# Two token blocks with attention beside them: where the scores lie, when the softmax and the stores run, and how early the next stage's weights are loaded

## The chip, the core and the metric

The kernel runs on one core of one Trainium2 chip. Its engines are TensorE (PE in the profile, its weight loads PEld), VectorE (DVE), ScalarE (ACT), GpSimd (POOL) and SyncE (SP, which issues nearly all DMAs here). The metric is the device time of one execution in microseconds (us), the median of several runs.

## The reference

Pooled attention, a gated layer and a second layer with a rational activation, all in float32:

```python
# q, k, v: 8 batches x 8 heads x 576 tokens x 64
k_p = k.reshape(B, H, Sp, 8, D).mean(axis=3)          # 72 pooled keys, v_p likewise
scores = scale * q @ k_p^T;  scores -= max(scores)
attn = exp(scores) / (sum(exp(scores)) + 1e-09)
x = (attn @ v_p)            # as 4608 tokens x 512
# gated layer, 512 -> 1536 -> 512
x = (silu(x @ w_gate) * (x @ w_val)) @ w_out
# second layer, 512 -> 2048 -> 512
h = x @ w_in;  P = a0 + a1 h + a2 h^2 + a3 h^3
Q = 1 + |b0||h| + |b1| h^2;  out = (P / (Q + 1e-06)) @ w_out2
```

## The kernel before, in words

The 4608 tokens are nine blocks of 512. The hidden width 1536 of the gated layer is twelve tiles `f` of 128. Every float32 product is done as three matmuls on a high and a low part (`mm3`), so a gate product `gp` or a value product `vp` of one tile is 12 matmuls of 128x512.

Stages in order of time: block 0 (35 to 158 us) also turns the weights into parts; blocks 1 and 2 (158.7 to about 355 us) run `gp` and `vp` for each tile; then three pairs of blocks run with fewer products (`ca`, `cb`, `cc`, 12 steps `n` each, to 775 us), which read sums of weights (`sw`) back from DRAM; then the output products, and from 950 us the second layer.

Attention for later blocks runs in between, in units of up to 128 tokens: block 2's during tiles 4 to 9 of block 1, that of blocks 3 and 4 during block 2. A unit goes: load `q` (`qload`); scores `sc` on PE; in the next tile the softmax read on DVE (`soft1`, L380 and L383, twice), the exponential on ACT (`soft_exp`, L393), sum and division (`soft2`, L405 to L408; the division on DVE or, with `helped`, on GpSimd), a copy (`soft3`, L416, GpSimd); in the tile after that PE transposes the result (`t`, L433 and L437), ACT and DVE copy it (`ptr` L440 and L445, `pt` L441), and PE multiplies by the pooled values (`pv`, L461 and L464), which ACT copies to `xraw` (L470).

The order is written by hand. `attention_slots` puts each step into a `plan` by tile and place; the loop over tiles calls the places: "0" ahead of `gp`, "A" behind the silu (L789), "B" ahead of the gated product `hh * vp` (L803), "B2" behind its store (L811), "C" at the end. All engines take their instructions in that order, so an instruction that waits holds up what stands behind it on its engine, and on SP a store that waits holds up the loads behind it. `prepare(2)` loads pieces of `k` and `v` and reduces them (L291, L309) in the same tile. `sum_weights`, `sum_splits` and `sum_store` work every second tile on the weight sums of the pair stage (`rs`, `ws`, stores `sd`, `wd`, `vd`). `stream(n, ...)` loads the pieces `sw` of step `n`; `token_sums` and `token_part` make the parts `x0b11`, `x0t1`, ... of the first pair on DVE and ACT.

PSUM has eight banks: four `ps_acc` (block 0's outputs, later the pair products), two `ps_gv` (`gp` and `vp`), two `ps_at` (scores, transposes and `pv` take turns). SBUF slots of 36 (`wslot`) hold weights and much else and are handed on as they come free.

Of the kernel before, what the change touches and what calls it, by code (L numbers as in the profile page):

```python
# [19 lines left out]
P = 128  # L20
# [44 lines left out]
def attention_gated_rational(  # L65
# [279 lines left out]

    SCALE = 1.0 / (POOL * math.sqrt(D))

    def scores(u, qt, early=False, helped=False, heads=False):

        b, s, n, o = u
        kr = st["kr", b]
        if early:
            w = wslot(f"p{b}_{s}", (P, 2 * 512), F32)
            pt = w[:, : H * SP].rearrange("p (h s) -> p h s", s=SP)
            pr = w[:, H * SP : H * SP + 6 * RG].rearrange("p (c r i s) -> p c r i s", c=2, r=3, i=2)
        else:
            pt = at.tile([P, H, SP], F32, tag="p", name=f"p{b}_{s}", bufs=2)  # L360
            pr = at.tile([P, 2, 3, 2, REST], F32, tag="pr", name=f"pr{b}_{s}")
        mx = at.tile([P, 2, NPAIR], F32, tag="mx", name=f"mx{b}_{s}", bufs=2)
        sm = at.tile([P, H], F32, tag="sm", name=f"sm{b}_{s}", bufs=2)
        banks = []
        for half in range(2):
            sc = bank(f"sc{b}_{s}_{half}", min(s // P, 2) if early else None)
            banks.append(sc[:, : 4 * SP].rearrange("p (c s) -> p c s", s=SP))

        for c in range(NPAIR):
            for half in range(2):  # L370
                rows = slice(half * D, (half + 1) * D)
                nc.tensor.matmul(  # L372
                    banks[half][:n, c, :], qt[rows, c * n : (c + 1) * n], kr[rows, c * SP : (c + 1) * SP],
                    start=True, stop=True,
                )

        def soft1():
            for half in range(2):
                sc = banks[half]
                nc.vector.tensor_reduce(mx[:n, half], sc[:n], axis=AX.X, op=ALU.max)  # L380
                if heads:
                    continue
                nc.vector.tensor_tensor(  # L383
                    pt[:n, half::2], sc[:n],
                    mx[:n, half].unsqueeze(2).to_broadcast([n, 4, SP]), op=ALU.subtract,
                )

# [98 lines left out]
    def attention_slots(js, start, helped=False, heads=False):  # L486


        def put(slot, place, fn):
            plan.setdefault((slot, place), []).append(fn)  # L490

        groups = [g for j in js for g in units(j)]
        owner = [j for j in js for g in units(j)]
        box = {}
        fl = [(g, i) for g in range(len(groups)) for i in range(len(groups[g]))]

        def do_xraw(j):
            if j > PLAIN and (j - PLAIN) % 2:
                st["xraw", j] = [wslot(f"xraw{j}_{i}", (P, 2, BLK), F32) for i in range(2)]
            else:  # L500
                t = keep.tile([P, KT, BLK], F32, tag="xraw", name=f"xraw{j}")
                st["xraw", j] = [t[:, 0:2, :], t[:, 2:4, :]]
        for n, (g, i) in enumerate(fl):
            u = groups[g][i]
            slot = start + n
            put(slot - 1, "B2", lambda u=u: box.__setitem__(("q", u), qload(u)))
            put(slot, "C", lambda u=u: box.__setitem__(("s", u), scores(u, box.pop(("q", u)), False, helped, heads)))
            put(slot + 1, "A0" if slot + 1 >= PLAIN * NF1 else "0", lambda u=u: box["s", u][0]())
            put(slot + 1, "0" if heads else "A", lambda u=u: box["s", u][1]())
            put(slot + 1, "B" if js[0] >= PLAIN else "B2", lambda u=u: [fn() for fn in box.pop(("s", u))[2:]])  # L510

            def t_(u=u, g=g, i=i, at_bank=0 if slot + 2 >= PLAIN * NF1 else None):
                if i == 0:
                    box["pt", g] = new_pt(f"{js[0]}_{g}")
                for fn in transposes(u, box["pt", g], i * P, at_bank):
                    fn()
            put(slot + 2, "A", t_)
            if i + 1 == len(groups[g]):
                def v_(g=g):
                    j = owner[g]  # L520
                    if ("xraw", j) not in st:
                        do_xraw(j)
                    values(groups[g], box.pop(("pt", g)), st["xraw", j])
                    if g + 1 < len(groups) and groups[g + 1][0][0] != groups[g][0][0]:
                        build_vs(groups[g + 1][0][0])
                put(slot + 2, "B", v_)
# [104 lines left out]

    def sum_weights(f):

        rg, rv = sums_w[f] = [ldp.tile([P, 2, QUART], F32, tag="ld", name=f"r{x}{f}") for x in "gv"]
        for r, w in zip((rg, rv), (W1[f"g{f}"], W1[f"v{f}"])):
            nc.vector.tensor_tensor(r.rearrange("p h c -> p (h c)"), f32(w[:, 0, :]), f32(w[:, 1, :]), op=ALU.add)
        (a11, a12), (a21, a22) = ([r[:, h] for h in range(2)] for r in (rg, rv))
        nc.gpsimd.tensor_tensor(a11, a11, a21, op=ALU.subtract)
        nc.gpsimd.tensor_tensor(a21, a21, a22, op=ALU.add)
        nc.gpsimd.tensor_tensor(a22, a22, a11, op=ALU.subtract)  # L640
        nc.gpsimd.tensor_tensor(a12, a12, a22, op=ALU.subtract)
# [109 lines left out]

    LOW_LAST = ((0, 0), (0, 1), (1, 0))
    acc = alloc_acc(0)
    h_t = {}

    def out_mm(f):
        ht = h_t.pop(f)
# [14 lines left out]
    for j in range(PLAIN):  # L772
        for f in range(NF1):
            slot = (j - 1) * NF1 + f
            place(j, f, "0")
            if (j, f) in begin:
                todo += prep_jobs(begin[j, f])
            run = prepare(2)
            if j == 2:
                second.begin(turns(f - NF1), turns(f - NF1 + 1))  # L780
            if j and slot % 2 == 0:
# [1 line left out]
            g_w, v_w = W1[f"g{f}"], W1[f"v{f}"]  # L783
            if j == 0:
                first.step(6)
            gp = ps_gv.tile([P, BLK], F32, tag="gv", name=f"gp{j}_{f}")
            mm3(gp, [(g_w, slice(kk * P, (kk + 1) * P), x[kk], full) for kk in range(KT)], order=LOW_LAST)
            hh = hp.tile([P, BLK], F32, tag="hh", name=f"hh{j}_{f}", bufs=2)
            nc.scalar.activation(hh, gp, AF.Silu)  # L789
            place(j, f, "A")  # L790
            if j == 0:
# [2 lines left out]
                sum_splits(slot // 2)  # L794
            if slot > 0 and slot % 2 == 0:
                sum_store(slot // 2 - 1)
            vps = ps_gv.tile([P, BLK], F32, tag="gv", name=f"vp{j}_{f}")
            mm3(vps, [(v_w, slice(kk * P, (kk + 1) * P), x[kk], full) for kk in range(KT)], order=LOW_LAST)
            if j == 2:
                second.middle()  # L800
# [3 lines left out]
            if j == 0:  # L804
# [2 lines left out]
                first.step(6)  # L807
                low_part(ht[:, 1, :], hh, ht[:, 0, :])
                h_t[f] = ht
            else:  # L810
                nc.sync.dma_start(h_d[0, f][:, j - 1, :], hh)  # L811
            place(j, f, "B2")
            if j == 0 and f:
                out_mm(f - 1)
            if j == 2:
# [2 lines left out]
            if j == 1 and f == NF1 - 2:  # L818
                nxt, convs = convert_x(st.pop(("xraw", 2)), "x2", True)
                for c_ in convs:  # L820
                    c_()
            if j == 2 and f == NF1 - 2:
                token_sums(0, nc.vector)
                stream(0, 1, 0, 2, 3)
                token_part(0, "b11")
        if j == 0:
            first.finish()
# [54 lines left out]
        nc.sync.dma_start(t, h_d[p, k])  # L882

    sum_store(NF1 - 1)
    second.paired = True
    token_part(0, "t1")
    begin_chain(0)
    token_part(0, "t2")
    stream(1, 1, 0, 2)
    for n in range(full_n):  # L890
        p, f = divmod(n, NF1)
        stage = PLAIN + p
# [342 lines left out]
```

## Time and profile before

| | us |
|---|---|
| median of 3 runs (1796.48 to 1797.9) | 1797.1 |
| the profiled execution, its own time | 1793.78 |
| its span | 1792.0 |
| PE busy | 1737.4 (97%) |
| DVE busy | 1402.7 (78%) |
| ACT busy | 1147.0 (64%) |
| GpSimd busy | 293.1 (16%) |

The mean granted clock of TensorE is 0.992 of full speed. The span is shorter than the execution by 1.78 us, which lie around it. In the page's 40 slices of 44.8 us PE is at nine tenths or more in all but the first, the fifth, the seventh and the ninth; the last three lie in blocks 1 and 2 and where the pair stage begins. DMA is at nine tenths or more for a longer time in the pair stage alone.

In rows of the timeline the first number is the start in us, the second the busy time; then engine, line, operation, tile written and tiles read, shapes and count; in brackets the idle time before it and what ended that.

### The profile page before, as it was taken

How to read it: one execution, taken by the hardware profiler on the slowest of the kernel's cores; microseconds unless marked ns; L12 is line 12 of the kernel's file. 1: busy time of each engine (PE TensorE's matmuls, PEld its weight loads, DVE VectorE, ACT ScalarE, POOL GpSimd, SP SyncE). 2: the span in 40 equal slices, each digit the busy share in tenths (PEclk: the TensorE clock that was granted, in tenths of full speed). 3: DMA queues.
4: the chain of work that ended last, by engine and by line, in shares of the span. 5: the costliest groups of instructions: out<-in, count | busy, mean ns of one | idle time of the engine just before them, and what ended most of it. 6: DMA issues, size and time to landing. Idle time of an engine off the chain costs nothing.

```text
span 1792.0 us, 23733 instructions
## 1 busy us (share of the span) xinstructions
PE 1737.4 (97%) x8176; PEld 1424.1 (79%) x8176; DVE 1402.7 (78%) x2303; ACT 1147.0 (64%) x2014; POOL 293.1 (16%) x396
## 2 busy tenths in 40 slices
PE   6999898989999999999999999999999999999999
PEld 5777677768878888878888888888888888888887
DVE  7985666757776764467777799989898989898987
ACT  6784455556767754345555577776777777776775
POOL 3443224415545442200000000000000000000000
PEclk9999999989999999999999999999999999999999
DMA  7833655789999989998236701010000000000000
GB/s 286 296 125 131 222 192 198 260 312 352 386 347 344 372 300 356 384 380 312 88 128 223 267 1 48 1 48 18 30 24 24 24 24 24 24 24 24 1 24 24
DMA packets 132505, 297.87 MB, mean 166 GB/s; under 512 B 12960, under 2 KB 54560, under 8 KB 131360
## 3 DMA queue, kind: packets, MB, share of 16 engines
q1 hardware_dynamic: 131520, 295.75, 45.5%
q8 instruction: 65, 1.06, 0.2%
q10 hardware_dynamic: 864, 0.60, 0.1%
q14 instruction: 56, 0.46, 0.1%
HBM read 200.87 MB, written 95.42 MB: 165 GB/s over the span
## 4 chain that ended last, share of the span: by engine, by line
PE 81%; DVE 6%; ACT 4%; DMA 4%; issue 2%; POOL 1%; SPq 1%; DVEq 0%; POOLq 0%; ACTq 0%
PE acco L260 22%; PE h L260 22%; PE ca L260 9%; PE ya L1078 7%; PE cc L260 5%; PE yc L1078 4%; PE cb L260 2%; PE yb L1078 2%; PE gp L260 2%; PE vp L260 2%; DMA v<-in_v 1%; PE sc L372 1%; PE pv L461 1%; DMA sw<-sd 1%; ACT L393 1%
## 5 line engine op out<-in xcount | busy, mean ns | idle before, releaser
L260 PE MATMUL h<-z,wi 128*128 128x512 f32 x1728 | 414.6, 389 | 0.0
L260 PE MATMUL acco<-wo,gt 128*128 128x512 f32 x1728 | 414.6, 389 | 0.0
L260 PEld LDWEIGHTS h<-z,wi 128*128 128x128 f32 x1728 | 324.4, 188 | 67.4
L260 PEld LDWEIGHTS acco<-wo,gt 128*128 128x128 f32 x1728 | 324.3, 188 | 67.3
L1144 ACT ACTIVATE sq<-h 128x512 f32<-128x512 f32 x144 | 85.8, 596 | 175.2 <-PE h L260 175.0
L1151 DVE SCALAR_TENSOR_TENSOR w<-sq,neg,w 128x512 f32<-128x512 f32 x144 | 108.0, 750 | 43.0 <-ACT w L1145 42.9
L260 PE MATMUL vp<-x,wv 128*128 128x512 f32 x432 | 113.3, 411 | 1.3 <-ACT hh L789 0.7
L1161 DVE SCALAR_TENSOR_TENSOR g<-t,neg,e 128x512 f32<-128x512 f32 x144 | 108.3, 752 | 5.1
L1165 ACT ACTIVATE gt<-g 128x512 fp32r<-128x512 f32 x144 | 90.9, 631 | 32.9 <-DVE g L1161 32.9
L1148 ACT ACTIVATE t<-h,neg 128x512 f32<-128x512 f32 x144 | 111.8, 776 | 0.0
L1157 DVE SCALAR_TENSOR_TENSOR t<-t,neg,h 128x512 f32<-128x512 f32 x144 | 107.7, 748 | 5.1
L1158 DVE SCALAR_TENSOR_TENSOR e<-w,ln 128x512 f32<-128x512 f32 x144 | 98.6, 685 | 13.5 <-ACT ln L1155 13.5
L260 PE MATMUL gp<-x,wg 128*128 128x512 f32 x432 | 108.2, 397 | 0.8 <-DVE wg L94 0.8
L1155 ACT ACTIVATE ln<-ln,lnb 128x512 f32<-128x512 f32 x144 | 104.3, 724 | 4.7
L1145 ACT ACTIVATE w<-h,cab 128x512 f32<-128x512 f32 x144 | 98.4, 684 | 8.2 <-DVE e L1158 8.1
L1159 DVE SCALAR_TENSOR_TENSOR e<-e,ln 128x512 f32<-128x512 f32 x144 | 99.7, 692 | 5.0
L1166 DVE TENSOR_TENSOR gt<-g,gt 128x512 fp32r<-128x512 f32 x144 | 98.9, 687 | 2.2 <-ACT gt L1165 0.8
L260 PEld LDWEIGHTS vp<-x,wv 128*128 128x128 f32 x432 | 83.6, 198 | 21.4 <-DVE wv L94 2.8
L1156 DVE TENSOR_TENSOR t<-t,h 128x512 f32<-128x512 f32 x144 | 98.3, 683 | 0.0
L260 PEld LDWEIGHTS gp<-x,wg 128*128 128x128 f32 x432 | 79.0, 188 | 20.0 <-DVE wg L94 2.8
L1154 ACT ACTIVATE ln<-w 128x512 f32<-128x512 f32 x144 | 91.5, 635 | 0.2 <-DVE w L1151 0.2
L909 DVE TENSOR_TENSOR cc<-cq,ca 128x512 f32<-128x512 f32 x36 | 25.0, 694 | 61.6 <-PE ca L260 61.6
(264 smaller groups left out, 3178.5 us busy)
## 6 DMA issues: line engine op xcount, KB each, us to landing
sw<-sd SPq DMA_DIRECT2D x72, 512.0 KB, 6.8
sw<-wd SPq DMA_DIRECT2D x36, 512.0 KB, 6.8
h<-hq SPq DMA_DIRECT2D x36, 512.0 KB, 6.9
sd<-ws SPq DMA_DIRECT2D x24, 512.0 KB, 5.0
hl<-h SPq DMA_DIRECT2D x24, 512.0 KB, 6.7
hr<-h SPq DMA_DIRECT2D x24, 512.0 KB, 9.5
sw<-vd SPq DMA_DIRECT2D x36, 256.0 KB, 6.1
out<-ob SPq DMA_DIRECT2D x36, 256.0 KB, 2.2
```

The lines of the kernel that those rows point to most:

```text
L260: nc.tensor.matmul(acc, st[:, lw, cols], mv[:, rw, mcols], start=first and i == 0, stop=last and i == n - 1, skip_group_check=seeded,)
L1078: nc.tensor.matmul(banks[q], w[:, lw, cols], t[:, rw, :], start=opened and k == 0 and m == 0, stop=k == NK - 1 and m == 2, skip_group_chec ...
L1145: nc.scalar.activation(w0, hps, AF.Abs, scale=cab[:, 4:5])
L1148: nc.scalar.activation(t, hps, AF.Identity, scale=neg[:, 3:4], bias=neg[:, 2:3])
L1151: nc.vector.scalar_tensor_tensor(w0, sq, neg[:, 5:6], w0, op0=ALU.mult, op1=ALU.add)
L1155: nc.scalar.activation(ln, ln, AF.Exp, scale=-1.0, bias=lnb)
L1156: nc.vector.tensor_tensor(t, t, hps, op=ALU.mult)
L1157: nc.vector.scalar_tensor_tensor(t, t, neg[:, 1:2], hps, op0=ALU.add, op1=ALU.mult)
L1158: nc.vector.scalar_tensor_tensor(e, w0, C1, ln, op0=ALU.add, op1=ALU.mult)
L1159: nc.vector.scalar_tensor_tensor(e, e, 2.0, ln, op0=ALU.subtract, op1=ALU.mult)
L1161: nc.vector.scalar_tensor_tensor(g, t, neg[:, 0:1], e, op0=ALU.add, op1=ALU.mult)
L1166: lambda gt=gt, g=g: nc.vector.tensor_tensor(gt[:, 1, :], g, f32(gt[:, 0, :]), op=ALU.subtract),
```

## The change

Scores of tiles 12 to 34 (counted from block 0) go to the `ps_acc` banks. The exponential of those units stands at "0", ahead of the tile's silu. Sum and division of block 2's units stand at "B", ahead of the gated product. `hh` is kept in slots of two tiles, and two tiles' stores are issued together at the end of the second tile after them. `gp` and `vp` of the last two tiles of block 2 use `ps_acc`. `prepare` reduces in blocks 1 and 2 what it loaded one tile earlier. The weight sums lie in a slot `rs` of their own. Step 0's pieces are loaded at tiles 8 and 9 of block 2, two of step 1's at tile 10.

```diff
-            sc = bank(f"sc{b}_{s}_{half}", min(s // P, 2) if early else None)
+            sc = bank(f"sc{b}_{s}_{half}", min(s // P, 2) if early else at_bank)
...
+            plain = NF1 <= slot < PLAIN * NF1 - 1
+            at_bank = 2 if plain else None
+            put(slot, "C", lambda u=u, at_bank=at_bank: box.__setitem__(
+                ("s", u), scores(u, box.pop(("q", u)), False, helped, heads, at_bank)))
...
-            put(slot + 1, "0" if heads else "A", lambda u=u: box["s", u][1]())
-            put(slot + 1, "B" if js[0] >= PLAIN else "B2", lambda u=u: [fn() for fn in box.pop(("s", u))[2:]])
+            put(slot + 1, "0" if heads or plain else "A", lambda u=u: box["s", u][1]())
+            put(slot + 1, "B" if slot >= NF1 else "B2", lambda u=u: [fn() for fn in box.pop(("s", u))[2:]])
...
-        rg, rv = sums_w[f] = [ldp.tile([P, 2, QUART], F32, tag="ld", name=f"r{x}{f}") for x in "gv"]
+        r = wslot(f"rs{f}", (P, 2, 2, QUART), F32)
+        rg, rv = sums_w[f] = [r[:, i] for i in range(2)]
...
+    def store_plain(slot):
+        j, f = slot // NF1 + 1, slot % NF1
+        nc.sync.dma_start(h_d[0, f][:, j - 1, :], h2[j, f // 2][:, f % 2, :])
...
-            run = prepare(2)
+            run = prepare(2, j > 0)
...
+            pool, tag = (ps_acc, "acc") if j == 2 and f >= NF1 - 2 else (ps_gv, "gv")
...
+                if f % 2 == 0:
+                    h2[j, f // 2] = wslot(f"hh{j}_{f}", (P, 2, BLK), F32)
+                hh = h2[j, f // 2][:, f % 2, :]
...
-            else:
-                nc.sync.dma_start(h_d[0, f][:, j - 1, :], hh)
             place(j, f, "B2")
+            if j and slot % 2 == 0 and slot:
+                store_plain(slot - 2)
+                store_plain(slot - 1)
...
+            if j == 2 and f == NF1 - 4:
+                stream(0, 1, 0)
+            if j == 2 and f == NF1 - 3:
+                stream(0, 2, 3)
             if j == 2 and f == NF1 - 2:
                 token_sums(0, nc.vector)
-                stream(0, 1, 0, 2, 3)
+                stream(1, 1, 0)
...
-    stream(1, 1, 0, 2)
+    stream(1, 2)
```

Lines move with it: the silu L789 is L803, the gated product L803 is L817, the store L811 is L762, the loads `sw` L743 are L747.

ACT in block 2, tile 1, before (`hh2_1` is the silu of block 2's tile 1, `p2_512` the exponential of a unit, `ws6` the split of a weight sum):

```order
L789 ACT_TABLE_LOAD
L789 ACTIVATE hh2_1_2636<-gp2_1_2623 128x512
L440 ACTIVATE ptr3_0_2639<-t12_384_2645 96x2x128
L441 ACTIVATE pt3_0_2638<-t02_384_2640 128x4x128
L393 ACT_TABLE_LOAD
L393 ACTIVATE p2_512_2598<-p2_512_2598 64x576
L97 ACTIVATE ws6_0_2652<-rv6_2548 128x512
L97 ACTIVATE ws6_1_2653<-rg6_2547 128x512
```

The same after:

```order
L393 ACT_TABLE_LOAD
L393 ACTIVATE p2_512_2584<-p2_512_2584 64x576
L117 ACTIVATE rawi2_0_0_2531<-rawi2_0_0_2531 128x256
L118 ACTIVATE rawi2_0_0_2531<-rawi2_0_0_2531 128x256
L803 ACT_TABLE_LOAD
L803 ACTIVATE hh2_0_2553<-gp2_1_2610 128x512
L440 ACTIVATE ptr3_0_2625<-t12_384_2631 96x2x128
L441 ACTIVATE pt3_0_2624<-t02_384_2626 128x4x128
L97 ACTIVATE ws6_0_2637<-rs6_2533 128x512
L97 ACTIVATE ws6_1_2638<-rs6_2533 128x512
```

The exponential and its table load now stand ahead of the silu and its table load; `ptr` and `pt`, the copies of the transposes, come behind both.

DVE in block 1, tile 7, before (`ws3` the split, `kr3` the reduced keys, `hh1_7` the gated product, then sum and division of unit `p2_128`):

```order
L445 TENSOR_TENSOR ptr2_1_2218<-t12_0_2224,ptr2_1_2218 32x2x128
L94 SCALAR_TENSOR_TENSOR ws3_0_2231<-rv3_2096,ws3_0_2231 128x512
L94 SCALAR_TENSOR_TENSOR ws3_1_2232<-rg3_2095,ws3_1_2232 128x512
L291 TENSOR_REDUCE kr3_2090<-k3_1024_2198 128x64
L291 TENSOR_REDUCE kr3_2090<-k3_1536_2200 128x64
L803 TENSOR_TENSOR hh1_7_2215<-hh1_7_2215,vp1_7_2237 128x512
L405 TENSOR_REDUCE sm2_128_2183<-p2_128_2180 128x8
L406 TENSOR_SCALAR sm2_128_2183<-sm2_128_2183 128x8
L407 RECIPROCAL sm2_128_2183<-sm2_128_2183 128x8
L408 TENSOR_TENSOR p2_128_2180<-p2_128_2180,sm2_128_2183 128x576
```

The same after:

```order
L445 TENSOR_TENSOR ptr2_1_2208<-t12_0_2214,ptr2_1_2208 32x2x128
L94 SCALAR_TENSOR_TENSOR ws3_0_2220<-rs3_2087,ws3_0_2220 128x512
L94 SCALAR_TENSOR_TENSOR ws3_1_2221<-rs3_2087,ws3_1_2221 128x512
L291 TENSOR_REDUCE kr3_2082<-k3_0_2083 128x64
L291 TENSOR_REDUCE kr3_2082<-k3_512_2085 128x64
L405 TENSOR_REDUCE sm2_128_2173<-p2_128_2170 128x8
L406 TENSOR_SCALAR sm2_128_2173<-sm2_128_2173 128x8
L407 RECIPROCAL sm2_128_2173<-sm2_128_2173 128x8
L408 TENSOR_TENSOR p2_128_2170<-p2_128_2170,sm2_128_2173 128x576
L817 TENSOR_TENSOR hh1_6_2107<-hh1_6_2107,vp1_7_2226 128x512
```

The gated product now comes behind the sum and the division, and the keys reduced are those loaded a tile earlier.

SP from tile 9 to tile 10 of block 2, before (`sd10`, `wd10`, `vd10` stores of weight sums, `h0_10` the store of the gated product just made, `q4_256` the load of a unit, `sw0` the first pair step's weights):

```order
L651 DMA sd10_0_519<-ws10_0_3404 128x1024
L651 DMA sd10_1_520<-ws10_1_3405 128x1024
L652 DMA wd10_485<-wg10_1499 128x1024
L653 DMA vd10_497<-wv10_1536 256x1x256
L811 DMA h0_10_551<-hh2_10_3470 128x512
L276 DMA q4_256_3493<-in_q 128x512
L743 DMA sw0_1_3507<-sd0_0_499 128x1024
L743 DMA sw0_0_3509<-wd0_475 128x1024
L743 DMA sw0_2_3511<-sd0_1_500 128x1024
L741 DMA sw0_3_3513<-vd0_487 128x2x256
L276 DMA v5_3_3521<-in_v 128x512
```

The same after:

```order
L747 DMA sw0_2_3422<-sd0_1_500 128x1024
L745 DMA sw0_3_3424<-vd0_487 128x2x256
L276 DMA v5_1_3426<-in_v 128x512
L276 DMA v5_2_3428<-in_v 128x512
L204 DMA i2_1_parts_445<-rawi2_1_0_3282 256x1x256
L655 DMA sd10_0_519<-ws10_0_3383 128x1024
L655 DMA sd10_1_520<-ws10_1_3384 128x1024
L656 DMA wd10_485<-wg10_1499 128x1024
L657 DMA vd10_497<-wv10_1536 256x1x256
L276 DMA q4_256_3473<-in_q 128x512
L762 DMA h0_8_549<-hh2_8_3304 128x512
L762 DMA h0_9_550<-hh2_8_3304 128x512
```

The pieces of `sw0` have moved ahead of the stores of `sd10`, and no store of a product that was just made stands ahead of `q4_256`; the stores behind it are those of tiles 8 and 9.

## Rows read from the trace of the kernel before

**Rows 1.** Stretches: length; busy PE, PEld, DVE, ACT, POOL; granted clock; DMA share; GB/s.

```profile
260.00:366.00 106.00, 92.73 (x497) 73.67 (x495) 67.64 (x137) 58.87 (x95) 39.73 (x60) 0.94 0.62 217
366.00:517.00 151.00, 143.04 (x754) 115.10 (x753) 107.48 (x203) 98.84 (x186) 69.36 (x94) 0.98 0.98 360
328.00:392.00 64.00, 52.17 (x232) 40.05 (x232) 41.18 (x79) 34.15 (x59) 16.57 (x25) 0.89 0.82 290
...
410.00:420.00 10.00, 10.00 (x55) 8.19 (x54) 7.65 (x17) 6.59 (x13) 2.38 (x4) 1.00 1.05 405
```

**Rows 2.** PE waits, 158.5 to 366 us: engine, line, releaser, total us, times, longest.

```profile
PE t L433 <- DVE p L383: 10.3, 5, 3.0
PE sc L372 <- DMA q<-in_q: 5.5, 4, 2.9
```

**Rows 3.** PE timeline, blocks 1 and 2: start, busy us, instructions, wait in brackets.

```profile
180.49 2.88 PE L260 MATMUL gp<-x,wg 128*128 128x512 f32 x12
...
222.16 4.57 PE L260 MATMUL vp<-x,wv 128*128 128x512 f32 x12
...
236.23 2.98 PE L260 MATMUL gp<-x,wg 128*128 128x512 f32 x12
...
255.62 3.06 PE L260 MATMUL gp<-x,wg 128*128 128x512 f32 x12
...
268.80 0.43 PE L433 MATMUL t<-ident,p 64*128 64x64 f32 x4 [2.70 <-DVE p L383]
...
335.25 2.88 PE L260 MATMUL gp<-x,wg 128*128 128x512 f32 x12
```

**Rows 4.** GpSimd timeline beside the wait at 268.80.

```profile
268.35 0.46 POOL L416 COPY pr<-p 64x96 f32<-64x96 f32 x2
```

**Rows 5.** DVE timeline, tiles 5 and 6 of block 2.

```profile
306.39 0.69 DVE L94 SCALAR_TENSOR_TENSOR ws<-rv,ws 128x512 fp32r<-128x512 f32 x1 [2.51 <-ACT ws L97]
...
311.27 0.45 DVE L380 TENSOR_REDUCE mx<-sc 128x4 f32<-128x288 f32 x1
...
313.06 0.68 DVE L636 TENSOR_TENSOR rg<-wg 128x512 f32<-128x512 f32 x1
...
314.37 0.42 DVE L445 TENSOR_TENSOR ptr<-t,ptr 32x256 fp32r<-32x256 f32 x1
315.86 0.68 DVE L309 TENSOR_REDUCE vp<-v 96x64 f32<-96x512 f32 x1 [1.07 <-DMA v<-in_vrest]
...
318.51 0.45 DVE L380 TENSOR_REDUCE mx<-sc 128x4 f32<-128x288 f32 x1
```

**Rows 6.** ACT timeline, tile 7 of block 2.

```profile
317.62 0.43 ACT L117 ACTIVATE rawo<-rawo 128x256 f32<-128x256 f32 x1 [0.98 <-DMA rawo<-in_wo]
...
320.45 0.60 ACT L789 ACTIVATE hh<-gp 128x512 f32<-128x512 f32 x1 [0.77 <-PE gp L260]
...
321.39 0.58 ACT L441 ACTIVATE pt<-t 128x512 f32<-128x512 f32 x1
321.99 1.28 ACT L393 ACT_TABLE_LOAD   x1
323.29 0.68 ACT L393 ACTIVATE p<-p 128x576 f32<-128x576 f32 x1
323.88 0.61 ACT L97 ACTIVATE ws<-rv 128x512 fp32r<-128x512 f32 x1
```

**Rows 7.** PE timeline, from tile 10 of block 2 into the pair stage.

```profile
343.94 2.93 PE L260 MATMUL gp<-x,wg 128*128 128x512 f32 x12
...
357.94 1.39 PE L372 MATMUL sc<-kr,q 64*128 64x72 f32 x16 [2.92 <-DMA q<-in_q]
360.40 2.90 PE L260 MATMUL ca<-x0b,sw 128*128 128x512 f32 x6 [1.07 <-DMA sw<-wd]
...
377.79 2.93 PE L260 MATMUL ca<-x0b,sw 128*128 128x512 f32 x6 [5.63 <-DMA sw<-wd]
...
382.93 1.12 PE L372 MATMUL sc<-kr,q 64*128 64x72 f32 x16
```

More of the change, by code (lines that the diff above doesn't have):

```diff
@@ L346, in attention_gated_rational, with scores @@
     SCALE = 1.0 / (POOL * math.sqrt(D))
-    def scores(u, qt, early=False, helped=False, heads=False):
+    def scores(u, qt, early=False, helped=False, heads=False, at_bank=None):
         b, s, n, o = u
@@ L506, in attention_slots @@
             put(slot - 1, "B2", lambda u=u: box.__setitem__(("q", u), qload(u)))
-            put(slot, "C", lambda u=u: box.__setitem__(("s", u), scores(u, box.pop(("q", u)), False, helped, heads)))
+            plain = NF1 <= slot < PLAIN * NF1 - 1
+            at_bank = 2 if plain else None
+            put(slot, "C", lambda u=u, at_bank=at_bank: box.__setitem__(
+                ("s", u), scores(u, box.pop(("q", u)), False, helped, heads, at_bank)))
             put(slot + 1, "A0" if slot + 1 >= PLAIN * NF1 else "0", lambda u=u: box["s", u][0]())
-            put(slot + 1, "0" if heads else "A", lambda u=u: box["s", u][1]())
-            put(slot + 1, "B" if js[0] >= PLAIN else "B2", lambda u=u: [fn() for fn in box.pop(("s", u))[2:]])
+            put(slot + 1, "0" if heads or plain else "A", lambda u=u: box["s", u][1]())
+            put(slot + 1, "B" if slot >= NF1 else "B2", lambda u=u: [fn() for fn in box.pop(("s", u))[2:]])
             def t_(u=u, g=g, i=i, at_bank=0 if slot + 2 >= PLAIN * NF1 else None):
@@ L753, in attention_gated_rational @@
     acc = alloc_acc(0)
-    h_t = {}
+    h_t, h2 = {}, {}
+    def store_plain(slot):
+        j, f = slot // NF1 + 1, slot % NF1
+        nc.sync.dma_start(h_d[0, f][:, j - 1, :], h2[j, f // 2][:, f % 2, :])
     def out_mm(f):
@@ L785, in attention_gated_rational @@
                 first.step(6)
-            gp = ps_gv.tile([P, BLK], F32, tag="gv", name=f"gp{j}_{f}")
+            pool, tag = (ps_acc, "acc") if j == 2 and f >= NF1 - 2 else (ps_gv, "gv")
+            gp = pool.tile([P, BLK], F32, tag=tag, name=f"gp{j}_{f}")
             mm3(gp, [(g_w, slice(kk * P, (kk + 1) * P), x[kk], full) for kk in range(KT)], order=LOW_LAST)
-            hh = hp.tile([P, BLK], F32, tag="hh", name=f"hh{j}_{f}", bufs=2)
+            if j == 0:
+                hh = hp.tile([P, BLK], F32, tag="hh", name=f"hh{j}_{f}", bufs=2)
+            else:
+                if f % 2 == 0:
+                    h2[j, f // 2] = wslot(f"hh{j}_{f}", (P, 2, BLK), F32)
+                hh = h2[j, f // 2][:, f % 2, :]
             nc.scalar.activation(hh, gp, AF.Silu)
@@ L796, in attention_gated_rational @@
                 sum_store(slot // 2 - 1)
-            vps = ps_gv.tile([P, BLK], F32, tag="gv", name=f"vp{j}_{f}")
+            vps = pool.tile([P, BLK], F32, tag=tag, name=f"vp{j}_{f}")
             mm3(vps, [(v_w, slice(kk * P, (kk + 1) * P), x[kk], full) for kk in range(KT)], order=LOW_LAST)
@@ L884, in attention_gated_rational @@
     sum_store(NF1 - 1)
+    store_plain(2 * NF1 - 2)
+    store_plain(2 * NF1 - 1)
     second.paired = True
```

## The prediction

> **What bounds the kernel now.** I read the stages first, then PE's waits, then the timelines of the engines beside the longest waits. PE is the bound over the whole span, but not in blocks 1 and 2 and where the pair stage begins: in 260 to 366 us PE is busy 92.73 of 106 us at a granted clock of 0.94, DVE 67.64, ACT 58.87, and DMA has room at 0.62. In 366 to 517 us PE is busy 143.04 of 151, with DMA at 0.98 [rows 1]. No engine is full in blocks 1 and 2, so the limit there is a chain across engines.
>
> PE's waits name it. Of the time to 366 us, 10.3 us in five waits stand before the transposes `t`, ended by the softmax read L383 (it frees the bank that scores and transposes share); 5.5 us in four stand before the scores, ended by a load of `q` [rows 2]. A third cost follows such waits: the value product at 222.16 takes 4.57 us for the 12 matmuls that take 2.9 elsewhere [rows 3], so the clock is low right after them; 6 matmuls take 2.90 at 360.40 and 12 take 2.93 at 343.94 [rows 7].
>
> Where a bank wait is removed, what is late next? At 268.80 the transposes begin [rows 3]; the copy L416 of the softmax result on GpSimd, which the second half of the same transposes reads, ends at 268.35 + 0.46 = 268.81 [rows 4]. So the softmax itself is about as late as the bank, and new banks alone would give almost nothing there. What counts is how early the softmax comes and how long DVE and ACT need for a tile.
>
> **The change part by part.**
>
> *Softmax ahead of the silu, division ahead of the product.* No instruction is added on DVE, ACT or PE (70 table loads on ACT both times); the order decides. After the change the loop of a tile runs: gated product, softmax read (DVE), exponential, the words of a raw weight (odd tiles), table load, silu, `ptr`, `pt`, `ws` (ACT, odd tiles), then DVE up to the next product. Behind the exponential, which waits for the softmax read, stand the silu and `pt` on ACT; PE's `pv` waits for `pt`, DVE's product for the silu.
> An odd tile: softmax read 313.06 - 311.27 = 1.79 [rows 5]; exponential 323.88 - 323.29 = 0.59; two word copies of 0.43, pipelined, 0.8; table load 323.29 - 321.99 = 1.30; silu and `ptr` 321.39 - 320.45 = 0.94; `pt` 0.60; one `ws` of 0.61 before DVE may go on [rows 6]; DVE from the `ws` to the end of the product 311.27 - 306.39 = 4.88 [rows 5]. Sum 11.5. The exponential's own table load lies beside the softmax read.
> An even tile has no words and no `ws`: 1.79 + 0.59 + 1.30 + 0.94, then DVE from `ptr` to the product's end, 318.51 - 314.37 - 1.07 of waiting = 3.07, and 0.3 to 0.6 more where there are two reductions [rows 5]: 8.0. Two tiles: 19.5.
> Before, the eight tiles 1 to 8 of block 2 take 335.25 - 255.62 = 79.6 [rows 3], 19.9 for two. After: 4 x 19.5 = 78.0. **Term B: -1.6.** So most of the bank wait comes back as other waits: `pt` now comes behind the exponential and two table loads' worth of ACT, and by this walk PE waits 0.6 to 3.4 us before `pv` in six tiles (10 us together), where it now waits before `t`.
> Block 1, tiles 4 to 9: 236.23 - 180.49 = 55.74 [rows 3]. Tile 5 has no transposes yet, so its loop lacks 0.9; with two pairs at 18.6 and tiles 4 and 9 at 7.2 (PE's own) it is 51.6. **Term A: -4.1**, and 0.9 more from the wait for `q` at tile 11. Ends: 0 if the loop stays, -8.9 if all its waits and the slow clock behind them go.
>
> *Stores two tiles later, loads one tile ahead of their reductions.* The same stores and loads, none added. In the order before, the store of a product just made stands on SP ahead of the next `q`, `k`, `v`, so these go out only after the product, and DVE waits for them: 1.07 before the reduction at 315.86 [rows 5]. After it SP never waits for a fresh product, and a reduction's data has a tile (8 us) more. That is in the 3.07 above. It costs two tile slots and two load buffers held longer; where a slot came late, the next user would wait for a store, none to 3 us; I take none, since the slots asked for in block 2 were given back tiles before.
>
> *Boundary: `sw` of step 0 at tiles 8 and 9, of step 1 at tile 10.* Before, from tile 10's `gp` at 343.94 to the scores at 382.93 PE takes 38.99, with waits of 2.92 for `q`, 1.07 and 5.63 for `sw` and 6 matmuls in 2.9 us after them [rows 7]. PE's own work there: four products of 12 at 2.8, scores 1.05, seven groups of 6 at 1.4: 22.0. After, `q` and `sw` are asked for 8 to 16 us earlier. Then DVE is late: eight token sums and the low parts of `x0b11` and `x0t1`, with the last tiles' own work between them, end about 16 us after tile 10's begin, and PE wants them at 13.5; I put 3.4 on it: 25.4. **Term C: -13.6.** Ends: 0 (DMA takes as long as before) and -17.0.
>
> *Allowance.* +3 for the slow clock after the new waits at `pv` (a product of 4.57 for 2.9 after a wait near 3 us, two or three of them), bounds 0 and +8. +2 for DMA at the boundary: 290 GB/s x 64 us = 18.6 MB from 328 to 392 us now have to pass in about 50 us, 371 GB/s; the rows show 405 in 410 to 420 us and 360 over 366 to 517 [rows 1], so between 46 and 52 us, bounds -0 and +6.
> The Trainium skill ("DMA: Bandwidth & Descriptors", Specifications) gives about 358 GB/s from HBM for a core. By that the boundary would take 52 us and the allowance be some 2 us higher; the 405 of this trace is above it, so I go by the row.
> The Trainium skill ("ScalarE: Activation LUTs", Rules for kernel authors) counts 2.7 us for each change of table set. By that the load between exponential and silu would add 1.4 to every tile, the pair would be 22.3 and the change would lose in the blocks what it wins at the boundary; the trace has 1.30 from load to activation, so this gets no chance of its own.
>
> *Downstream.* The pair stage's order is unchanged; PE is busy 95% there [rows 1], so an earlier begin is kept.
>
> **Sum.** -1.6 - 4.1 - 0.9 - 13.6 + 3 + 2 = -15.2, on the profiled execution's 1793.78 (span 1792.0 and 1.78 around it): 1778.6. The median of the runs is 3.3 above that execution: 1797.1 - 15.2 = 1781.9; I say 1781.
>
> **Rivals.**
> 1. *All waits in the blocks go.* If exponential and loads slip beside PE's products, A gives -8.9, B -9 (the waits before `t` and the slow products behind them), C -17 + 2: about -33, 1764. For it: DVE and ACT are busy under two thirds of the time in blocks 1 and 2. Against: the loop of 19.5, which is made of rows and serial by the order.
> 2. *The boundary is bound by DMA.* `sw`, `q` and stores come at DMA's pace whenever they are asked for: C falls to -3, the sum to about -6, 1791. For it: DMA share 0.98 right behind. Against: 0.62 ahead of it, which is where the loads go.
> 3. *The banks were the wait in the blocks and the new order costs nothing*, or the reverse, *A and B give nothing*: -9 to -20, inside the forecast's range.
> 4. *Slower: the exponential stalls ACT.* ACT takes its instructions in order. If it is still busy with the last tile's copies when the softmax read ends, the table load (1.30) is no longer hidden, and silu, `pt`, `ws` are all late by it. It is hidden as long as ACT is free 0.5 us (1.79 - 1.30) after the product's end; from there each further delay counts in full. In the ten more of the thirteen tiles with an exponential that is +13.0, and with `pt` late by the whole 3.2 (0.59 + 2 x 1.30) instead of 1.7 in six tiles +9: -15.2 + 22.0 = +6.8, 1803.9. For it: ACT copies `pv` at the end of a tile. Against: three of the thirteen by my walk, not all.
>
> **How the numbers follow.** Forecast 0.60 (1781, own range 1772 to 1789), rival 1 0.15 (1764), rival 2 0.12 (1791), rival 3's outer ends 0.05, rival 4 0.08 (1804). A measurement tells about 0.2%, 3.6 us, from no change: faster is below 1793.5. Rival 2 reaches over that with a third, 0.04; rival 4 is slower but for 0.02. Faster 0.88, same 0.05, slower 0.07. The range leaves out half of rival 1, rival 4 and little else: 1765 to 1793.
>
> **What would show it.** Right: from tile 10's `gp` to the second scores of the pair stage some 25 us, with no wait of over 1 us for `sw` or `q` there, and the wait in `ca` of 5.63 gone; PE's waits before `t` shorter but `pv` waiting for `pt` in about six tiles; tiles 1 to 8 of block 2 still 77 to 79 us. Rival 1: these tiles in 70. Rival 2: waits of `ca` for `sw` again, DMA share 1.0 from tile 8 on. Rival 4: ACT's table load ahead of the exponential begins after the softmax read has ended, in most tiles. I'd be wrong in the main if C is under 8 us, or if the two blocks get longer.

## The result, and the profile after

| | before | after |
|---|---|---|
| median, us (6 runs each) | 1796.89 | 1781.53 |
| lowest and highest | 1794.8, 1800.18 | 1778.77, 1784.16 |
| ratio of the runs, 95% interval | | 0.9912 [0.9898, 0.9926] |
| span of the profiled run | 1792.0 | 1777.0 |

The change takes 15.4 us off the median; 1781 was forecast. Where it comes from, by PE's timeline (the begin of the gate product `gp` of a tile to the begin of another's; the last row ends at the second scores of the pair stage):

| stretch | before | forecast | after |
|---|---|---|---|
| A: block 1, tiles 4 to 9 | 55.74 | 51.6 | 52.91 |
| block 1, tiles 10 and 11 | 13.05 | 12.2 | 12.11 |
| B: block 2, tiles 1 to 8 | 79.63 | 78.0 | 78.64 |
| C: tile 10 of block 2 to the second scores | 38.99 | 25.4 (27.4 with its allowance) | 29.69 |

A, the two tiles behind it, B and C give 2.8 + 0.9 + 1.0 + 9.3 = 14.0 of the 15.0 between the two spans. Another 1.4 lies ahead of block 1, in stages that the change does not touch: `gp` of its first tile begins at 157.31 for 158.72. In the profiled runs of the experiments it begins anywhere from 157.28 to 158.92, so this part is run to run. From the begin of block 1 to tile 10 of block 2 the time falls by 4.8; 3.0 of it is PE's own busy time (168.75 to 165.71), the rest waits. Behind the second scores nothing is given back: they begin 15.5 earlier, the output products 15.4.

PE's timeline after, to be read against [rows 3]:

```profile
179.07 2.88 PE L260 MATMUL gp<-x,wg 128*128 128x512 f32 x12
...
231.98 2.98 PE L260 MATMUL gp<-x,wg 128*128 128x512 f32 x12
...
250.41 3.06 PE L260 MATMUL gp<-x,wg 128*128 128x512 f32 x12
...
281.09 0.66 PE L433 MATMUL t<-ident,p 128*128 128x128 f32 x4 [2.08 <-POOL p L408]
...
281.72 4.59 PE L260 MATMUL vp<-x,wv 128*128 128x512 f32 x12
...
329.05 2.88 PE L260 MATMUL gp<-x,wg 128*128 128x512 f32 x12
```

The starts give 231.98 - 179.07 = 52.91 and 329.05 - 250.41 = 78.64. A wait of 2.08 before `t` is still there, now ended by GpSimd's division, and the `vp` behind it takes 4.59, as such products did in [rows 3].

PE's waits from 158.5 to 366 us (total, times, longest), against [rows 2]:

```profile
PE pv L461 <- ACT pt L441: 9.6, 5, 3.5
PE sc L372 <- DMA q<-in_q: 3.5, 1, 3.5
PE t L433 <- POOL p L408: 3.4, 4, 2.1
PE t L433 <- DVE p L408: 1.3, 1, 1.3
```

The softmax read is gone as a releaser of `t`, and so are three of the four waits for `q`; in their place `pv` waits for `pt`. The sum of PE's waits up to tile 10 of block 2 hardly changes (16.2 before, 14.7 after); that is why A and B gave so little.

The boundary, against [rows 7]:

```profile
337.72 2.93 PE L260 MATMUL gp<-x,wg 128*128 128x512 f32 x12
...
352.29 1.12 PE L372 MATMUL sc<-kr,q 64*128 64x72 f32 x16 [3.48 <-DMA q<-in_q]
353.33 2.81 PE L260 MATMUL ca<-x0b,sw 128*128 128x512 f32 x6
355.93 2.00 PE L260 MATMUL cc<-x0t,sw 128*128 128x512 f32 x6
...
359.76 2.11 PE L260 MATMUL cb<-x0b,sw 128*128 128x512 f32 x6 [0.45 <-ACT x0b L97]
...
363.09 1.52 PE L260 MATMUL ca<-x0b,sw 128*128 128x512 f32 x6
365.53 1.95 PE L260 MATMUL ca<-x0t,sw 128*128 128x512 f32 x6 [0.91 <-ACT x0t L97]
367.41 1.12 PE L372 MATMUL sc<-kr,q 64*128 64x72 f32 x16
```

The waits for `sw` (1.07 and 5.63) are gone, and `ca` at 363.09 runs at once; the wait for `q` is not: 3.48 for 2.92. Behind each wait the groups of six matmuls are slow: 2.81 and 2.00 behind the wait for `q`, 2.11 and 1.95 behind the two short ones, where 1.52 is the time at 363.09. The granted clock is 0.53 from 353.33 to 355.90, near the lower of its two levels (1.2 and 2.4 GHz), and 0.89 from 352.29 to 367.41. The chain that ended last tells why `q` is late (start, length, what):

```profile
336.95 7.35 DMA sw<-sd
...
344.32 0.74 SPq L657
...
345.11 7.04 DMA q<-in_q
...
352.29 1.12 PE sc L372 x16
```

A piece of `sw` that SP asked for at 336.95 landed 7.35 later; the store `vd` (L657) behind it waited for that landing (SP itself stood 0.5 us there), then the load of `q` went out at 345.11 and took 7.04 to land. The DMA engines are full there:

```profile
328.00:354.00 26.00, 25.11 (x117) 20.20 (x117) 17.81 (x35) 14.72 (x26) 13.61 (x20) 1.00 0.70 246
328.00:354.00 26.00, 22.48 (x114) 18.36 (x113) 19.58 (x36) 9.08 (x18) 7.72 (x12) 0.99 1.02 374
```

The first row is before, the second after (columns as in [rows 1]): 1.02 of their time at 374 GB/s in 328 to 354 us, for 0.70 at 246. The loads were asked for earlier, and they queue.

ACT in tile 6 and 7 of block 2 shows the new order, against [rows 6]:

```profile
312.15 1.28 ACT L393 ACT_TABLE_LOAD   x1 [4.95 <-DVE p L383]
313.44 0.69 ACT L393 ACTIVATE p<-p 128x576 f32<-128x576 f32 x1
...
314.78 1.28 ACT L803 ACT_TABLE_LOAD   x1
316.07 0.60 ACT L803 ACTIVATE hh<-gp 128x512 f32<-128x512 f32 x1
...
316.83 0.59 ACT L441 ACTIVATE pt<-t 128x512 f32<-128x512 f32 x1
```

ACT is idle 4.95 us until the softmax read has ended and loads the exponential's table at 312.15; the silu comes at 316.07 behind a second load. PE's `pv` waited 2.93 for the `pt` at 316.83. DVE waits in turn for `ptr` behind the silu in all of tiles 1 to 8; before and after:

```profile
DVE ptr L445 <- ACT ptr L440: 7.3, 5, 2.3
DVE ptr L445 <- ACT ptr L440: 23.8, 8, 4.9
```

Its waits for `ws` fall from 10.3 to 2.3 in the same tiles.

### The profile page after: what moved, and what is told of

It is laid out like the page before. It is cut to its first block, busy times and chain, and to the rows that moved or that the text cites. A ratio compares the mean times of both kernels' runs of the same rounds, so it can differ in the third digit from the quotient of the medians.

```text
span 1777.0 us, 23705 instructions
## 1 busy us (share of the span) xinstructions
PE 1729.2 (97%) x8176; PEld 1417.5 (80%) x8176; DVE 1403.9 (79%) x2303; ACT 1145.1 (64%) x2014; POOL 294.2 (17%) x396
## 4 chain that ended last, share of the span: by engine, by line
PE 81%; DVE 7%; ACT 6%; DMA 3%; issue 2%; POOL 2%; SPq 0%; DVEq 0%; POOLq 0%; ACTq 0%
PE acco L260 22%; PE h L260 22%; PE ca L260 10%; PE ya L1099 7%; PE cc L260 5%; PE yc L1099 4%; PE cb L260 2%; PE vp L260 2%; PE yb L1099 2%; PE gp L260 2%; PE pv L461 1%; PE sc L372 1%; ACT L803 1%; DMA sw<-sd 1%; DVE p L383 1%
## 5 line engine op out<-in xcount | busy, mean ns | idle before, releaser
L260 PE MATMUL vp<-x,wv 128*128 128x512 f32 x432 | 109.3, 400 | 0.7 <-DVE wv L94 0.4
```

The lines of the kernel that those rows point to most:

```text
L260: nc.tensor.matmul(acc, st[:, lw, cols], mv[:, rw, mcols], start=first and i == 0, stop=last and i == n - 1, skip_group_check=seeded,)
```

## The experiments

All times are medians of 4 to 10 runs, with the ratio to the kernel before in the same session. A, B and C are the stretches above, read from one profiled run each. B differs by 1.4 (e7) and 2.1 (e10) from that of e2 where the edit does not reach it, so about 2 us in B alone show nothing.

| run | A | B | C | median | ratio [95%] |
|---|---|---|---|---|---|
| before | 55.74 | 79.63 | 38.99 | 1796.89 | 1 |
| after | 52.91 | 78.64 | 29.69 | 1781.53 | 0.9912 [0.9898, 0.9926] |
| e1 late streams | 52.96 | 78.68 | 34.20 | 1785.11 | 0.9931 [0.9909, 0.9953] |
| e2 exponential behind silu | 49.69 | 74.74 | 28.47 | 1771.56 | 0.9856 [0.9837, 0.9874] |
| e3 shared banks | 52.93 | 80.56 | 28.47 | 1781.42 | 0.9910 [0.9891, 0.9928] |
| e4 loads in their tile | 54.57 | 78.34 | 32.66 | 1784.07 | 0.9926 [0.9908, 0.9944] |
| e5 before, streams alone | 55.33 | 79.74 | 36.04 | 1793.98 | 0.9989 [0.9979, 0.9998] |
| e6 stores at once | 54.63 | 79.33 | 31.62 | 1786.62 | 0.9942 [0.9919, 0.9965] |
| e7 e2, `q` ahead | 49.73 | 76.13 | 28.14 | 1773.10 | 0.9870 [0.9854, 0.9886] |
| e8 e2, shared banks | 55.41 | 78.94 | 27.77 | 1779.49 | 0.9910 [0.9894, 0.9926] |
| e9 e2, sum ahead | 49.06 | 73.15 | 27.81 | 1772.34 | 0.9876 [0.9861, 0.9890] |
| e10 e2, block 1's division late | 51.79 | 76.85 | 27.29 | 1773.86 | 0.9886 [0.9871, 0.9901] |
| e11 before, banks alone | 52.28 | 76.96 | 38.34 | 1788.35 | 0.9965 [0.9952, 0.9977] |
| e12 e2, sum ahead in odd tiles | 48.77 | 71.90 | 28.92 | 1769.61 | 0.9853 [0.9833, 0.9874] |

**e1, the weight loads late again.**

```diff
-            if j == 2 and f == NF1 - 4:
-                stream(0, 1, 0)
-            if j == 2 and f == NF1 - 3:
-                stream(0, 2, 3)
...
-                stream(1, 1, 0)
+                stream(0, 1, 0, 2, 3)
...
-    stream(1, 2)
+    stream(1, 1, 0, 2)
```

> The changed kernel with the pair stage's weight pieces asked for where they were before (all of step 0 at tile 10 of block 2, step 1 behind the block). Theory: the boundary got shorter because these loads start 8 to 16 us earlier. Then the stretch from tile 10's gate product to the second scores of the pair stage goes from 29.7 us back to 36 to 39, with waits of ca for sw again, and the run is 7 to 9 us slower than the change, about 1789. Rival: stores that no longer hold up SP brought the boundary its gain. Then the stretch stays under 32 and the run within 3 us of the change. Blocks 1 and 2 ahead of tile 8 stay as they are by both.

C is 34.20, half of the way back, and the run 3.6 us slower. PE's timeline has both waits for `sw` again, 3.91 and 3.77 for the 1.07 and 5.63 of [rows 7]:

```profile
355.18 2.90 PE L260 MATMUL ca<-x0b,sw 128*128 128x512 f32 x6 [3.91 <-DMA sw<-wd]
...
368.96 2.93 PE L260 MATMUL ca<-x0b,sw 128*128 128x512 f32 x6 [3.77 <-DMA sw<-wd]
```

The scores at 350.15 do not wait for `q` now, and the DMA share in 328 to 354 us is 0.88: without the early pieces in the queue, `q` is there in time. So the early loads are worth 4.5 of the 9.3 in C; the 7 to 9 us that I expected of the run were too much. That the stores have the rest, as the rival said, does not follow: with the stores back (e6) C is 1.9 longer, with the reductions back (e4) 3.0.

**e2, the exponential back behind silu, `ptr` and `pt`.**

```diff
-            put(slot + 1, "0" if heads or plain else "A", lambda u=u: box["s", u][1]())
+            put(slot + 1, "0" if heads else "A", lambda u=u: box["s", u][1]())
```

> The changed kernel with the exponential back behind silu, ptr and pt. Theory: the tile's loop is a serial chain of DVE and ACT by either order. The 9.6 us that PE waits for pt before pv go, waits before the transposes come back in their place, tiles 1 to 8 of block 2 stay at 77 to 80 us (78.6 in the change), and the run is within 3 us of the change. Rival 1: those 9.6 us are a real price of the new order, and the run is 5 to 9 us faster. Rival 2: the new order is what gained in the blocks, and the run is 4 us or more slower.

10.0 us faster than the change, with an interval clear of it: rival 1, and more than its 5 to 9. A gets 3.2 shorter, B 3.9, C 1.2. The waits of `pv` for `pt` are gone and only a part comes back before `t` (8.1 for 4.7 in the change):

```profile
PE t L433 <- POOL p L408: 5.8, 5, 2.7
PE t L433 <- DVE p L408: 2.3, 2, 1.3
PE sc L372 <- DMA q<-in_q: 1.9, 1, 1.9
```

ACT in tile 4 of block 2:

```profile
277.43 1.28 ACT L803 ACT_TABLE_LOAD   x1
278.73 0.60 ACT L803 ACTIVATE hh<-gp 128x512 f32<-128x512 f32 x1
...
281.19 0.58 ACT L441 ACTIVATE pt<-t 128x512 f32<-128x512 f32 x1
281.80 1.28 ACT L393 ACT_TABLE_LOAD   x1
```

Here the silu (278.73) starts with no wait, `pt` follows the transposes, and the exponential's load (281.80) comes when the softmax read is already over, so neither waits. In tiles 1 to 8 DVE waits 7.7 us for `ptr`, for 23.8. With the exponential ahead ACT idles until that read, and everything that PE and DVE want from ACT stands behind it.

**e3, the scores in the shared banks.**

```diff
-            at_bank = 2 if plain else None
+            at_bank = None
```

> The changed kernel with the scores back in the two banks that transposes and pv use. Theory: the bank was last only by a fraction of a microsecond, so this costs 0 to 2 us over both blocks; waits of the transposes are then ended by the softmax read again. Rival: the bank was the wait, and tiles 4 to 9 of block 1 and 1 to 8 of block 2 get 4 us or more longer together.

Time as the change (0.1 us). A is the same, B 1.9 longer and C 1.2 shorter, and PE's waits move once more, from `pt` to banks and copies:

```profile
PE t L433 <- POOL pr L416: 3.8, 3, 2.4
PE t L433 <- DVE p L383: 3.7, 2, 2.4
PE pv L461 <- ACT pt L441: 2.8, 3, 2.1
```

With the exponential ahead the banks give nothing that these runs can tell.

**e4, loads reduced in the tile that asks for them.**

```diff
-            run = prepare(2, j > 0)
+            run = prepare(2)
```

> The changed kernel with k and v reduced in the tile that loads them, as before. Theory: DVE waits for the data again, about 1 us in each of some eight tiles, ahead of the gated product, so blocks 1 and 2 get 3 to 6 us longer. Rival: since SP no longer waits for a fresh product the loads are there anyway, and the run is within 2 us of the change.

2.5 us slower; A is 1.7 and C 3.0 longer, B the same. The intervals overlap, so the sign rests on the stretches. DVE does not wait 1 us in eight tiles: from tile 4 of block 1 to tile 8 of block 2 it waits for no load at all, and why A is longer stays open. Two waits for `k`, 6.0 us together, stand at the begin of block 1, where PE loses nothing by them (tiles 0 to 3 take 21.78 for 21.76). Those that count stand at the boundary:

```profile
342.44 0.42 DVE L291 TENSOR_REDUCE kr<-k 128x32 f32<-128x256 f32 x1 [4.32 <-DMA k<-in_k]
...
358.40 1.46 DVE L309 TENSOR_REDUCE vp<-v 128x64 f32<-128x512 f32 x2 [2.25 <-DMA v<-in_v]
```

Behind the second, DVE gets to the parts `x0t` at 360.37, for 353.29 in the change.

**e5, the early loads alone, on the kernel before.** The diff is that of e1 the other way round.

> The kernel before with nothing but the earlier weight loads of the pair stage (step 0 at tiles 8 and 9 of block 2, two pieces of step 1 at tile 10). Late loads cost 4.5 us of the boundary's 9.3 in the changed kernel (34.2 for 29.7). Theory: the loads are worth the same alone; the boundary goes from 39.0 to 33 to 35, the wait for q stays or grows since that load still stands behind a fresh store, and the run is 4 to 6 us faster than before. Rival: with SP still held up by fresh stores, the loads do not get out earlier, and the gain is under 2 us.

1.6 us faster: the rival in size. C is 36.0. Its reason was not quite right: the pieces do get out earlier and PE no longer waits for `sw`, but the time is lost ahead of it. One product that never waited does now, for the gated product that holds its bank:

```profile
359.21 4.41 PE L260 MATMUL vp<-x,wv 128*128 128x512 f32 x12 [3.74 <-DVE hh L803]
```

The chain that ended last goes there through SP (start, length, what):

```profile
351.09 0.33 SPq L811
...
352.59 4.65 DMA v<-in_v
...
358.48 0.69 DVE hh L803
```

SP waits for tile 9's product to store it (L811), issues two pieces of `sw`, then the load of `v`; it lands 4.65 later, and DVE, which reduces it in this same tile, gets to tile 10's product at 358.48.

**e6, each product stored at once.**

```diff
+            if j:
+                store_plain(slot)
             place(j, f, "B2")
-            if j and slot % 2 == 0 and slot:
-                store_plain(slot - 2)
-                store_plain(slot - 1)
...
-    store_plain(2 * NF1 - 2)
-    store_plain(2 * NF1 - 1)
```

> The changed kernel with each gated product stored in its own tile, right behind the product, as before. Theory: SP waits for the product again and every q, k, v and sw behind it goes out later; since the reductions are a tile later the blocks hide it (A and B within 1 us), but q and sw at the boundary are late: 29.7 goes to 32 to 35, the run 3 to 5 us slower than the change. Rival 1: boundary bound by DMA alone: within 1.5 us of the change. Rival 2: the stores carry the gain of the blocks too: these get 3 us or more longer.

5.1 us slower, about what the theory forecast, with more waits for `q`:

```profile
...
PE sc L372 <- DMA q<-in_q: 7.1, 3, 4.5
```

7.1 us in three places, for 3.5 in one: 1.1 in A, 1.5 in tile 11 of block 1, 4.5 at the boundary. C is 1.9 longer. But the blocks do not hide the rest, as the theory said: A is 1.7 longer, the two tiles behind it 1.5, tile 0 of block 2 1.6 and B 0.7, 5.5 together. That is rival 2: the stores carry more of the blocks' gain than of the boundary's.

**e7, e2 with the load of `q` ahead.**

```diff
-            put(slot - 1, "B2", lambda u=u: box.__setitem__(("q", u), qload(u)))
+            put(slot - 1, "0" if slot == PLAIN * NF1 - 1 else "B2", lambda u=u: box.__setitem__(("q", u), qload(u)))
```

> The changed kernel with the exponential behind silu, ptr and pt (which alone gave 1771.6) and the load of q for the first scores of the pair stage moved ahead, from the end of tile 10's predecessor's order behind the stores of weight sums to the begin of that tile. Theory: q waits for its place in a full DMA queue; issued some 8 us earlier it is there, the wait of 1.9 (3.5 in the change) goes, and the boundary falls from 28.5 to 25 to 27: about 1769 to 1770. Rival: the DMA queue is full all the way, so the wait moves to sw or to the parts of x0, and the time stays within 1 us of 1771.6.

The wait for `q` is gone, C is 28.1 for 28.5 where the theory had 25 to 27, and the time is not less (1773.1 for 1771.6, intervals overlap). The rival: it is the parts of `x0` that PE waits for now,

```profile
PE cc L260 <- DVE x0t L94: 1.5, 1, 1.5
PE cb L260 <- ACT x0b L97: 1.3, 1, 1.3
```

the DVE and ACT chain that the prediction had put there.

**e8, e2 with the shared banks.** The diff is that of e2 and that of e3 together.

> The changed kernel with the exponential behind silu, ptr and pt and the scores back in the banks shared with transposes and pv. Theory: with this order PE's waits before the transposes are ended by the softmax result (8.1 us in all) and no longer by pt, and the softmax read is the earlier of the two; so the banks cost 0 to 2 us here as they did with the exponential ahead (1781.4 for 1781.5). Rival: with pt early, the bank becomes what the transposes wait for, and the run is 4 us or more slower than 1771.6.

7.9 us slower than e2, clear of its interval: the rival. A and B get 9.9 longer and the bank is again what the transposes wait for, by the softmax read that frees it:

```profile
PE t L433 <- DVE p L383: 10.6, 5, 3.1
```

That is the row of [rows 2] (10.3 in five) again.

**e9, e2 with sum and division right behind the exponential.**

```diff
-            put(slot + 1, "B" if slot >= NF1 else "B2", lambda u=u: [fn() for fn in box.pop(("s", u))[2:]])
+            put(slot + 1, "A" if plain else "B" if slot >= NF1 else "B2", lambda u=u: [fn() for fn in box.pop(("s", u))[2:]])
```

> The changed kernel with the exponential behind silu, ptr and pt (1771.6 by itself) and sum and division of every unit of blocks 1 and 2 right behind it, ahead of DVE's splits of weight sums and its reductions. In 1771.6's trace PE still waits 8.1 us before the transposes for the divided softmax, and DVE does its sum 1.2 to 3.5 us after the exponential ends. Theory: the softmax result is now the end of the loop, so these waits and the slow product behind one of them go: 6 to 9 us faster, 1763 to 1766, tiles 1 to 8 of block 2 at 69 to 72 us. Rival: DVE now waits for the exponential ahead of its other work, the gated product gets late instead, and the time is within 2 us of 1771.6.

Same time as e2: the rival. A and B are 2.2 shorter, tile 9 of block 2, which lies between B and C, is 2.7 longer. The waits for the softmax fall (from 8.1), and `vp` waits for the gated product that holds its bank:

```profile
PE t L433 <- POOL p L408: 4.9, 3, 2.4
PE vp L260 <- DVE hh L817: 4.3, 4, 1.9
```

**e10, e2 with block 2's units divided behind the product.**

```diff
-            put(slot + 1, "B" if slot >= NF1 else "B2", lambda u=u: [fn() for fn in box.pop(("s", u))[2:]])
+            put(slot + 1, "B" if js[0] >= PLAIN else "B2", lambda u=u: [fn() for fn in box.pop(("s", u))[2:]])
```

> The changed kernel with the exponential behind silu, ptr and pt, and block 2's units summed and divided behind the gated product again, as before the change (four units, all in block 1; DVE does the division there). Theory: the softmax result comes some 0.7 us later behind the product and the read ahead of the transposes with it, so tiles 4 to 9 of block 1 go from 49.7 to 51 to 53 us and the run is 1 to 3 us slower than 1771.6. Rival: the product is what matters there, coming 2 us earlier: same or faster.

2.3 us slower than e2, A 51.79 as forecast. The intervals touch, and B, which the edit does not reach, is 2.1 longer in this run too, so the size is not sure.

**e11, the kernel before with the new banks alone.**

```diff
-            sc = bank(f"sc{b}_{s}_{half}", min(s // P, 2) if early else None)
+            sc = bank(f"sc{b}_{s}_{half}", min(s // P, 2) if early else at_bank)
...
+            at_bank = 2 if NF1 <= slot < PLAIN * NF1 - 1 else None
```

> The kernel before with nothing but the scores in the four idle banks. By the step of the prediction that new banks alone give almost nothing, since the softmax copy is as late as the bank: within 2 us of before. Rival, by the comparison of shared and own banks with the exponential behind silu (1779.5 for 1771.6): the bank is what closes the loop in this order, and the run is 5 to 9 us faster than before, with PE's waits before t ended by GpSimd's p and no longer by the softmax read.

This edit changed part of what is computed, and which part I have not found out, so its time counts as a hint beside e8. It is 7.3 us faster than before, A by 3.5 and B by 2.7:

```profile
PE t L433 <- POOL p L408: 6.9, 5, 2.4
PE ca L260 <- DMA sw<-wd: 6.0, 2, 5.5
PE sc L372 <- DMA q<-in_q: 5.2, 4, 2.8
```

The bank wait (10.3) is gone and 9.0 of waits for the divided softmax stand there (2.1 of them ended by DVE's division), with the boundary's waits about as they were.

**e12, the sum behind the exponential in odd tiles alone.**

```diff
-            put(slot + 1, "A" if plain else "B" if slot >= NF1 else "B2", lambda u=u: [fn() for fn in box.pop(("s", u))[2:]])
+            put(slot + 1, "A" if plain and slot % 2 == 0 else "B" if slot >= NF1 else "B2", lambda u=u: [fn() for fn in box.pop(("s", u))[2:]])
```

> The changed kernel with the exponential behind silu, ptr and pt; sum and division stand right behind the exponential in odd tiles alone, where DVE is idle 2.5 us waiting for ws, and ahead of the gated product in even tiles as in the change. With them there in every tile (1772.3) PE's waits for the softmax fell from 8.1 to 4.9 us, but 4.3 us of waits of vp for the gated product came in. Theory: in odd tiles the sum fills idle time, in even tiles it held up the reductions; so most of the 4.3 goes, and the run is 2 to 5 us faster than 1771.6 and 1772.3, about 1768. Rival: the waits that are left change places once more, since DVE, ACT and GpSimd close one loop: within 1.5 us of 1772.

1769.6, the lowest of all and 11.9 under the change, but not to be told from e2 (0.9853 for 0.9856). B is the shortest, 71.9, but tile 9 behind it takes 10.7 for 8.6 in e2, so 2.1 of the 2.8 won in B are lost again, as the rival had it; of the softmax waits (8.1 in e2) and of the product's (4.3 in e9) these are left:

```profile
PE t L433 <- POOL p L408: 3.8, 3, 2.1
PE vp L260 <- DVE hh L817: 3.6, 4, 1.9
```

## Why the prediction was right, and which of its steps were not

*The loop of a tile (terms A and B): right in size.* Serial rows gave 78.0 for B and 78.64 was measured, 51.6 and 52.91 for A. The waits of `pv` for `pt` came as walked: 9.6 us in five places for 10 in six. The allowance of 3 for slow products was too much: two came (4.59 and 4.45 for 3.0), and the kernel before had three behind its own waits (4.57, 4.61 and 3.86). A and B together gave 3.8, where the forecast with its allowance was 2.7.

*"New banks alone would give almost nothing": wrong in the order it was said of.* I had compared one moment, 268.80, where bank and softmax copy were late together [rows 3, 4]. As I read it now, they are late together because they follow from each other: the bank frees late, so `t`, `ptr`, `pt`, the product and the next read are late too, and taking the bank away lets the whole loop slip back. e8 against e2 measures it at 7.9 us, with the exponential behind the silu as before and the other parts of the change in place; on the kernel before itself there is only the hint of e11. In the order of the change it is 0 (e3); that the loop closes through the exponential there is read from the waits of `pv` and `ptr`.

*The exponential ahead of the silu: the cost was in the walk, its meaning was not.* I priced the new loop rightly and wrote that most of the bank wait comes back, without seeing that this order was what brought it back. e2 shows it: 10 us with the new banks, where with the shared ones the order makes 1.9 (e3 and e8, intervals overlapping). So the change holds a gain of about 8 from the banks and gives as much away. Rival 4 named the place (silu and `pt` behind the exponential) with a wrong condition: the table load begins only behind the softmax read in three of thirteen units, as walked. What costs is ACT standing still for the read, whether the load is hidden or not. (The argument counts 70 table loads on ACT both times; the profiles have 75 both times, and only that the number is equal matters there.)

*The boundary (term C): right in direction, 2.3 less than with its allowance.* I had two causes of the end mixed up. I put 3.4 on DVE's parts and 2 on DMA; measured are 0.45 + 0.91 for the parts and 3.48 for `q`, behind a DMA queue at 1.02. So a piece of rival 2 is in the result. But the waits sum to 4.8 for the 5.4 that I put there; the term that was too small is PE's own work, 22.0 in the forecast and 24.9 measured. I took seven groups of six at 1.4, as if no wait came between them; they took 12.7 for 9.8, since those behind a wait came at a lower granted clock. That DVE's parts cost 2.0 less than I had put and `q` 1.5 more is luck where the two nearly cancel. The mark "no wait of over 1 us for `q`" failed, that of the 5.63 held. e7 then shows that the other limit stands right behind: with `q` there in time, the parts cost 1.48 + 1.31.

*Stores and loads: priced at nothing of their own, and worth 5 and 2 to 3.* I had put the stores into the loop as a condition (no DMA wait in the DVE rows). By e6 they carry about 5 us of the 15, by e1 the early weight loads 3.6, by e4 the later reductions 2.5. These are not shares to be added: e5 shows the weight loads alone at 1.6, since there they stand on SP between a store that waits and a load of `v` that DVE needs at once. By its chain they need the late stores or the late reductions beside them; no run has them with one of the two alone.

*Downstream: right.* 15.5 us at the second scores are 15.4 at the output products. That the total is hit within 1 us is in part luck: A and B gave 1.1 more than forecast, C 2.3 less, and 1.4 came from run to run ahead of block 1.

What stays open: which engine closes the loop in e12, where waits of 3 to 4 us are left in each of two places, and what e11's edit changed in the result. Three parts were never undone by themselves: the slot `rs` of the weight sums, the `ps_acc` banks for the products of the last two tiles, and, in the order of the change, sum and division ahead of the product.

By the limit of about 358 GB/s from HBM for a core that the Trainium skill gives ("DMA: Bandwidth & Descriptors", Specifications) the stretch from 328 to 354 us could not have run at 374 GB/s; the measurement decides. The queue was full at that rate, though (1.02), so my row of 405, read over 10 us, was no rate to count on over 26.

## What to carry to other kernels

Where two waits end within a microsecond of each other inside a loop, don't conclude that removing one gives nothing: follow each round the loop and see whether it causes the other. In an engine that takes its instructions in order, put behind everything else that is ready the one instruction that waits for another engine; a softmax moved "early" held up a silu whose input was there. And test the parts of a change that came together one by one: here one part took back what another had won, and without it the kernel is 10 us faster.

## What the runs showed of the hardware that was not expected

A load of 256 KB asked for while the DMA engines are full took 7.04 us from issue to landing; in 328 to 392 us the median of three such loads of `q` was 3.8 before the change and 7.0 after it. Asking for the weights earlier made the small load that PE needs first slower by 3.2, about the wait that was left (3.48).
